# Pairs' value products and scores moved behind the second layer of their step, squares of h in PSUM in all steps, block sums amid the next step's gelu

## The chip, the cores and the metric

One core of one Trainium2 chip runs the whole program. The metric is the device time of one execution in microseconds; lower is better.

## The reference, cut to what matters

Attention over a window of 16 positions plus block summaries (block maxima of the keys, block means of the values), and on its output a two-layer network with a rational activation.

```python
# B=4, H=8, S=768, D=64, blocks of 32, window 16; 3072 tokens, d_model 512, d_ff 2048, fp32
k_sum = k.reshape(B, H, nb, block, D).max(axis=3)
v_sum = v.reshape(B, H, nb, block, D).mean(axis=3)
scores = concat(masked scale*q@k.T, scale*q@k_sum.T + log(block))
x = softmax(scores) @ concat(v, v_sum)            # then tokens x 512
h = x @ w_in
P = a0 + a1*h + a2*h*h + a3*h*h*h
Q = 1.0 + |b0|*|h| + |b1|*h*h
out = (P / (Q + 1e-6)) @ w_out
```

## The kernel before, in words

**Tiles.** The attention is cut into 48 halves of 64 queries; from half 16 on they come in pairs. The network runs over 6 groups of 512 tokens, and for each over 16 chunks of 128 hidden units. One chunk of one group is a *step*, number n = 16 g + fc, 0 to 95. Products in fp32 precision are made of three fp32r products of a high and a low part.

**One step n.** TensorE makes `h` (12 matmuls of 512 columns, `moe1`, L515), then the second layer `po` of an older step, n - 3 (12 matmuls, `moe2`, L596). Between the two lies the activation `gelu` (L531) in parts named by letters, which the text uses with the step's number behind them (c42):

- a, on ScalarE: `sq` (square of h) and `ta` (|h| scaled); b, on ScalarE: `tu` (linear in h). In steps where `sq` has no tile of its own it is written to `tq` in SBUF.
- c, on VectorE: `tq` from `sq` and `ta` (this is Q); d, on ScalarE: `ta` = ln, then exp.
- e, f, on VectorE: `tu` times h, twice; both read h in PSUM. i: `gh` = `tu` times `ta`. j and J: `tq` from `tq` and `gh`, then `tu` from `tu` and `tq`. k, on GpSimd (POOL): `gl` = `tu` times `ta`.

**PSUM.** Four banks hold `po`; two (`ps_h`) hold `h` and, in steps with a pair, the pair's value products `av`; two (`ps_a`) hold the pair's two score tiles `sc` and the tiles `sq`. `ta`, `tq`, `tu` have two buffers in SBUF each.

**Pairs.** Steps 14, 18, 22, ..., 74 (`halves`) each carry a pair: `both_scores` makes its `sc` tiles; `softmax` takes them off with 8 VectorE rows (`ss<-sc,mask`), 8 exponentials on ScalarE, reciprocals on VectorE and 8 scalings on GpSimd; one step later two VectorE transposes (`tb`) and a way through DRAM turn them; four steps later `both_values` makes `av`, ScalarE copies it (`x`, `xh`) and `xl` is formed. The output of a group is copied off by ScalarE (`o`) in steps 18, 34, 50, 66.

**Block sums.** For batches 2 and 3 `reduces` holds 8 VectorE reductions each (4 `ks`, 4 `vs`), one a step, in steps 20 to 29 and 37 to 53.

**Order.** Up to step 13 the order is a table of tokens. From step 14 on (`NSTRICT`, L734) the loop at the end issues step by step; TensorE keeps that order to the instruction, and the other engines' order comes from a list scheduler that goes by priority. All engines run their instructions in the order in which they then stand. All instructions of the loop bear line 113, that of the helper that records them, in the profile.

Of the kernel before, what the change touches and what calls it, by code (L numbers as in the profile page):

```python
# [12 lines left out]
AF = mybir.ActivationFunctionType  # L13
ALU = mybir.AluOpType
# [5 lines left out]
BLK, WIN = 32, 16  # L20
# [45 lines left out]
NSTRICT = NFC - 2  # L66
# [8 lines left out]
SQ_PS = "011001101001110"  # L75
# [5 lines left out]
NHALF = NT // HQ  # L81
# [3 lines left out]
def tile_kernel(ctx, tc, qw_in, kraw, kwin, vpad, vred, wio, a, b, cmask, cident, cavg, out):  # L85
# [37 lines left out]
    pe, dve, act, gps, syn = (Kept(e) for e in (nc.tensor, nc.vector, nc.scalar, nc.gpsimd, nc.sync))  # L123
# [65 lines left out]
    def value_sum(bi, c):  # L189
        vs, vr = vsum[bi], sums.pop(("v", bi, c))  # L190
        tc.keep_in_program_order(dve.tensor_reduce(vs[:, c, :], vr, axis=AX.X, op=ALU.add))
        if c == NVC - 1:
            dve.tensor_scalar_mul(vs, vs, 1.0 / BLK)

    def value_tiles(bi):
        vt = []
# [36 lines left out]
    def att_load(jj):  # L233
        bi, j = divmod(jj, NJ)
        assert jj < HPG + 2 or jj >= 2 * HPG + 2 or jj - 2 in scored
        syn.dma_start(out=qw[jj % 2], in_=qw_in[bi, j])
        syn.dma_start(out=kw[jj % 2][:, 0:NKC - 1], in_=kwin[bi, j])
# [277 lines left out]
    def moe1(g, fc, xh, xl):  # L515
        h = ps_h.tile([P, GT], F32, tag="h", name=f"h{g}_{fc}")
        k = 0
        wt = weights(fc)
        for i, x in ((0, xh), (0, xl), (1, xh)) if 0 < g * NFC + fc < NFC else ((0, xh), (1, xh), (0, xl)):
            if k:  # L520
                yield
            assert ("w" if i else "wh", fc) in order
            for cc in range(NCC):
                pe.matmul(h, wt[:, i, 0, cc * P:(cc + 1) * P], x[:, cc, :], start=(k == 0), stop=(k == 3 * NCC - 1))
                k += 1
        gh = gp.tile([P, GT], F32R, tag="gh", name=f"gh{g}_{fc}")
        gl = gp.tile([P, GT], F32R, tag="gl", name=f"gl{g}_{fc}")
        gelus[g * NFC + fc] = gelu(h, gh, gl, g, fc)
        queue.append((g, fc, (gh, gl)))

    def gelu(h, gh, gl, g, fc):  # L531
        ta = mp.tile([P, GT], F32, tag="ta", bufs=NTA, name=f"ta{g}_{fc}")
        tq = mp.tile([P, GT], F32, tag="tq", bufs=NTQ, name=f"tq{g}_{fc}")
        tu = mp.tile([P, GT], F32, tag="tu", bufs=NTU, name=f"tu{g}_{fc}")
        n = g * NFC + fc
        sq = tq

        product = n < NSTRICT and PRODUCT[n] == "1"

        def a():  # L540
            nonlocal sq
            if product:
                act.activation(ta, h, AF.Abs)
                act.activation(tq, ta, AF.Identity, scale=cs[:, 5:6], bias=cs[:, 4:5])
                return
            if n < start_of(NHALF - 1) + 4 and (n not in halves if n > NSTRICT else n < len(SQ_PS) and SQ_PS[n] == "1"):
                sq = ps_a.tile([P, GT], F32, tag="a", name=f"sq{g}_{fc}")
            act.activation(sq, h, AF.Square)
            act.activation(ta, h, AF.Abs, scale=cs[:, 4:5])

        def b():
            act.activation(tu, h, AF.Identity, scale=cs[:, 3:4], bias=cs[:, 2:3])

        def c():
            if product:
                gps.tensor_tensor(tq, tq, ta, op=ALU.mult)
                return
            dve.scalar_tensor_tensor(out=tq, in0=sq, scalar=cs[:, 5:6], in1=ta, op0=ALU.mult, op1=ALU.add)

        def d():  # L560
            act.activation(ta, tq, AF.Ln, bias=cs[:, 7:8])
            act.activation(ta, ta, AF.Exp, scale=-1.0)

        def e():
            dve.tensor_tensor(tu, tu, h, op=ALU.mult)

        def f():
            dve.scalar_tensor_tensor(out=tu, in0=tu, scalar=cs[:, 1:2], in1=h, op0=ALU.add, op1=ALU.mult)

        def i():  # L570
            dve.scalar_tensor_tensor(out=gh, in0=tu, scalar=cs[:, 0:1], in1=ta, op0=ALU.add, op1=ALU.mult)

        def j():
            dve.scalar_tensor_tensor(out=tq, in0=tq, scalar=C1 * SH, in1=gh, op0=ALU.add, op1=ALU.mult)
            dve.scalar_tensor_tensor(out=tu, in0=tu, scalar=cs[:, 0:1], in1=tq, op0=ALU.add, op1=ALU.subtract)

        def k():
            gps.tensor_tensor(gl, tu, ta, op=ALU.mult)

        return dict(a=a, b=b, c=c, d=d, e=e, f=f, i=i, j=j, k=k)  # L580
# [6 lines left out]
        if not parts:  # L587
            del gelus[step]

    def gelu_rest(step):  # L590
        for what in "abcdefijk":
            if what in gelus[step]:
                gelus[step].pop(what)()
        del gelus[step]

    def moe2(fc, po, gh, gl):  # L596
        wt = weights(fc)
        for t in range(TPG):
            ts_ = slice(t * P, (t + 1) * P)
            for i, (l, r) in enumerate(((gh, 0), (gh, 1), (gl, 0))):  # L600
                pe.matmul(po[t], l[:, ts_], wt[:, r, 1, :], start=(fc == 0 and i == 0),
                   stop=(fc == NFC - 1 and i == 2))
            yield

    def finish(g, po):
        for t in range(TPG):
            if g == NG - 1:
                o = gp.tile([P, DM], F32, tag="gl" if t % 2 else "gh", name=f"o{g}_{t}")
            else:
                o = (gp if t in OWN else pp).tile([P, DM], F32, tag="o" if t in OWN else "p", name=f"o{g}_{t}", bufs=2 if t in OWN else 4)  # L610
            if g == NG - 1 and t == TPG - 1:
                rows = out[g * GT + t * P:g * GT + (t + 1) * P, :]
                o2 = gp.tile([P, DM], F32, tag="gh", name=f"o{g}_{t + 1}")
                act.copy(o[:, 0:DM // 2], po[t][:, 0:DM // 2])
                dve.tensor_copy(o2[:, 0:DM // 2], po[t][:, DM // 2:])
                act.dma_start(out=rows[:, 0:DM // 2], in_=o[:, 0:DM // 2])
                syn.dma_start(out=rows[:, DM // 2:], in_=o2[:, 0:DM // 2])
                continue
            if g == NG - 1 and t % 2:
                dve.tensor_copy(o, po[t])  # L620
            else:
                act.copy(o, po[t])
            syn.dma_start(out=out[g * GT + t * P:g * GT + (t + 1) * P, :], in_=o)

    queue, out_tiles, gelus = [], [], {}

    def second_layer():
        g, fc, r = queue.pop(0)
        assert g * NFC + fc not in gelus
        if fc == 0:  # L630
            out_tiles[:] = [ps_o.tile([P, DM], F32, tag="o", name=f"po{g}_{t}") for t in range(TPG)]
        yield from moe2(fc, out_tiles, *r)
        if fc == NFC - 1:
            with tc.high_priority(offset=80):
                finish(g, out_tiles)
# [11 lines left out]
    def lead(chain, all_of=False):  # L647
        for _ in chain or ():
            if not all_of:
                return  # L650

    def start_of(jj):
        return EARLY_HALF[jj - HPG] if jj < 2 * HPG else NFC - 2 + 4 * ((jj - 2 * HPG) // 2)

    halves = {}
    for jj in range(HPG, NHALF):
        halves.setdefault(start_of(jj), []).append(jj)
    reduces, loads = {}, {}
# [68 lines left out]
    for s in sorted(gelus):  # L727
        gelu_rest(s)
# [5 lines left out]
    for step in range(NSTRICT, NG * NFC + LAG):  # L734
        g, fc = divmod(step, NFC)
        if g < NG:
            lead(moe1(g, fc, *x32[g]), True)
        if step in gelus:
            with tc.high_priority(offset=-15):
                gelu_rest(step)  # L740
        with tc.high_priority(offset=40):
            if step - 4 >= NFC - 2 and halves.get(step - 4):
                both_values(halves[step - 4][0])
            for jj in halves.get(step, ()):
                key_blocks(jj)
            if step in halves:
                chain = [softmax(jj, sc) for jj, sc in zip(halves[step], both_scores(halves[step][0]))]
            else:
                chain = ()
            for _ in range(5):  # L750
                for c in chain:
                    lead(c)
            for jj in halves.get(step - CROSS, ()):
                if jj >= 2 * HPG:
                    crossed(jj)
            for jj in halves.get(step - 1, ()):
                if jj >= 2 * HPG:
                    load_v(jj)
            for jj in halves.get(step, ()):
                if jj + 2 < NHALF:  # L760
                    att_load(jj + 2)
        lead(second_layer(), True)
        for f, *args in reduces.get(step, []) + loads.get(step, []):
            f(*args)


# [56 lines left out]
```

## Time and profile before

| what | value |
|---|---|
| runs before, median of 3 (lowest, highest) | 637.39 us (636.9, 637.84) |
| profiled execution: span | 636.9 us |
| TensorE busy | 620.4 us, 97% |
| VectorE busy | 568.5 us, 89% |
| ScalarE busy | 457.1 us, 72% |
| GpSimd busy | 256.9 us, 40% |
| granted TensorE clock | full in all slices |

The profiled execution's own time is the lowest of the three, 636.9 us, and its span is the same: nothing lies around the span that the sum has to add. A busy share is an average over the span; matmuls overlap, so TensorE's own pace is read from the starts of its matmuls.

### The profile page before, as it was taken

The numbers are of one execution on the slowest core, as the hardware profiler recorded it, in microseconds if no ns is written. First come the engines' busy times: TensorE is split into PE (matmuls) and PEld (weight loads), VectorE is DVE, ScalarE is ACT, GpSimd is POOL, SyncE is SP. The second block draws the span as 40 slices with busy tenths as digits, with TensorE's granted clock in tenths as the row PEclk, the third lists the DMA queues.
The fourth block names the chain that finished last, engine by engine and source line by source line (L and its number), as shares of the span: only waits on it lengthen the run. The fifth ranks groups of instructions, "written<-read, shape, count | busy, mean of one in ns | idle before, by whom it ended". The sixth has DMA issues, their size and how long they took to land.

```text
span 636.9 us, 11880 instructions
## 1 busy us (share of the span) xinstructions
PE 620.4 (97%) x4078; PEld 494.2 (78%) x4078; DVE 568.5 (89%) x1155; ACT 457.1 (72%) x1020; POOL 256.9 (40%) x344
## 2 busy tenths in 40 slices
PE   8899999999999999999999999999999999999997
PEld 4466777778788878888888777888888888888886
DVE  5799999999898999889988989988988989898885
ACT  3789999877867757767767768667777765656662
POOL 1366679654434336233143244243234242222221
PEclk9999999999999999999999999999999999999999
DMA  9977777413434434324423433323333120100001
GB/s 289 341 281 233 242 220 232 165 40 126 148 113 136 138 114 155 106 99 138 134 89 120 136 124 101 95 72 106 93 132 100 57 65 1 63 4 1 1 2 66
DMA packets 51752, 77.66 MB, mean 122 GB/s; under 512 B 6260, under 2 KB 33524, under 8 KB 49772
## 3 DMA queue, kind: packets, MB, share of 16 engines
q1 hardware_dynamic: 50412, 74.75, 36.2%
q0 software_dynamic: 560, 1.77, 1.4%
q8 instruction: 32, 0.52, 0.3%
q10 hardware_dynamic: 720, 0.38, 0.2%
q14 instruction: 28, 0.23, 0.1%
HBM read 60.33 MB, written 14.73 MB: 118 GB/s over the span
## 4 chain that ended last, share of the span: by engine, by line
PE 62%; DVE 21%; ACT 6%; DMA 5%; issue 3%; POOL 2%; DVEq 0%; POOLq 0%; ACTq 0%
PE po L113 29%; PE h L113 28%; DVE tu L113 6%; DVE tq L113 5%; PE av L113 3%; DVE gh L113 2%; PE sc L113 2%; DMA wr<-in_wio_dram 2%; DVE wr L113 2%; ACT ta L113 2%; DMA kres<-in_kraw_dram 1%; DVE ss L113 1%; POOL ss L113 1%; DMA w<-wr 1%; ACT ss L113 1%
## 5 line engine op out<-in xcount | busy, mean ns | idle before, releaser
L113 POOL TENSOR_TENSOR gl<-tu,ta 128x512 fp32r<-128x512 f32 x96 | 129.4, 1348 | 296.5 <-DVE tu L113 140.3
L113 ACT ACTIVATE ta<-tq,cs 128x512 f32<-128x512 f32 x96 | 69.8, 727 | 80.5 <-DVE tq L113 79.6
L113 PE MATMUL po<-wearly,gh 128*128 128x512 f32 x384 | 120.3, 394 | 0.7 <-ACT o L113 0.7
L113 PE MATMUL po<-w,gh 128*128 128x512 f32 x384 | 119.7, 393 | 0.0
L113 POOL TENSOR_SCALAR ss<-ss,sm 128x120 f32<-128x120 f32 x176 | 84.3, 497 | 41.6 <-DVE sm L113 40.7
L113 PE MATMUL h<-xh,wearly 128*128 128x512 f32 x384 | 97.8, 394 | 1.6 <-DVE tu L113 1.0
L113 PE MATMUL h<-xh,w 128*128 128x512 f32 x384 | 96.8, 391 | 1.4 <-DVE sm L113 0.9
L113 PEld LDWEIGHTS h<-xh,wearly 128*128 128x128 f32 x384 | 71.5, 188 | 18.2 <-ACT ta L113 1.0
L113 PEld LDWEIGHTS po<-wearly,gh 128*128 128x128 f32 x384 | 70.8, 188 | 18.0 <-ACT o L113 2.4
L113 PEld LDWEIGHTS h<-xh,w 128*128 128x128 f32 x384 | 71.5, 188 | 17.0 <-ACT ta L113 1.3
L113 DVE SCALAR_TENSOR_TENSOR gh<-tu,cs,ta 128x512 fp32r<-128x512 f32 x96 | 73.8, 768 | 10.9 <-ACT ta L113 1.4
L113 PEld LDWEIGHTS po<-w,gh 128*128 128x128 f32 x384 | 71.2, 188 | 15.7 <-issue 1.1
L113 ACT ACTIVATE ss<-ss,sm 128x120 f32<-128x120 f32 x188 | 71.7, 385 | 12.2 <-DVE sm L113 12.2
L113 ACT ACTIVATE tu<-h,cs 128x512 f32<-128x512 f32 x96 | 74.7, 778 | 0.5 <-PE h L113 0.5
L113 PE MATMUL po<-w,gl 128*128 128x512 f32 x192 | 74.9, 390 | 0.0
L113 PE MATMUL po<-wearly,gl 128*128 128x512 f32 x192 | 74.8, 390 | 0.0
L113 DVE SCALAR_TENSOR_TENSOR tu<-tu,cs,tq 128x512 f32<-128x512 f32 x96 | 72.2, 753 | 2.6
L113 DVE SCALAR_TENSOR_TENSOR tu<-tu,cs,h 128x512 f32<-128x512 f32 x96 | 71.1, 741 | 2.2
L113 DVE SCALAR_TENSOR_TENSOR tq<-tq,gh 128x512 f32<-128x512 f32 x96 | 66.6, 694 | 2.7
L113 ACT ACTIVATE ta<-h,cs 128x512 f32<-128x512 f32 x95 | 64.6, 680 | 4.8 <-POOL gl L113 4.8
L113 DVE TENSOR_TENSOR tu<-tu,h 128x512 f32<-128x512 f32 x96 | 64.9, 676 | 0.1
L113 ACT ACTIVATE ta<-ta 128x512 f32<-128x512 f32 x96 | 60.8, 633 | 2.7
(92 smaller groups left out, 917.3 us busy)
## 6 DMA issues: line engine op xcount, KB each, us to landing
wr<-in_wio_dram SPq DMA_DIRECT2D x15, 1024.0 KB
cross<-tb SPq DMA_DIRECT2D x32, 256.0 KB
vw<-in_vpad_dram SPq DMA_DIRECT2D x42, 192.0 KB
kw<-in_kwin_dram SPq DMA_DIRECT2D x40, 192.0 KB
pts<-cross SPq DMA_DIRECT2D x96, 64.0 KB
out_dram<-o SPq DMA_DIRECT2D x23, 256.0 KB
qw<-in_qw_dram SPq DMA_DIRECT2D x40, 128.0 KB
kr<-in_kraw_dram SPq DMA_DIRECT2D x12, 384.0 KB
```

The source lines that it names most:

```text
L113: out = getattr(self.engine, name)(*args, **kw)
```

## The change

In the loop from step 14 on, the second layer now comes ahead of the pair's `both_values` and `both_scores`. `sq` gets a PSUM tile in every step after 14 (up to 77); in the step behind a pair, b comes first, then `ta`, and `sq` last. The block sums of step t are issued in step t + 1, between f and i. The scaling of the block means goes from VectorE to GpSimd.

```diff
         if c == NVC - 1:
-            dve.tensor_scalar_mul(vs, vs, 1.0 / BLK)
+            gps.tensor_scalar(vs, vs, 1.0 / BLK, 1.0, op0=ALU.mult, op1=ALU.mult)
...
-            if n < start_of(NHALF - 1) + 4 and (n not in halves if n > NSTRICT else n < len(SQ_PS) and SQ_PS[n] == "1"):
+            if n < start_of(NHALF - 1) + 4 and (n > NSTRICT or n < len(SQ_PS) and SQ_PS[n] == "1"):
                 sq = ps_a.tile([P, GT], F32, tag="a", name=f"sq{g}_{fc}")
-            act.activation(sq, h, AF.Square)
+            late = n > NSTRICT and n - 1 in halves
+            if not late:
+                act.activation(sq, h, AF.Square)
             act.activation(ta, h, AF.Abs, scale=cs[:, 4:5])
+            if late:
+                act.activation(sq, h, AF.Square)
...
-    def gelu_rest(step):
-        for what in "abcdefijk":
+    def gelu_rest(step, parts="abcdefijk"):
+        for what in parts:
             if what in gelus[step]:
                 gelus[step].pop(what)()
-        del gelus[step]
+        if not gelus[step]:
+            del gelus[step]
...
-        if step in gelus:
-            with tc.high_priority(offset=-15):
-                gelu_rest(step)
+        with tc.high_priority(offset=-15):
+            if step in gelus:
+                gelu_rest(step, "bacdef" if step - 1 in halves else "abcdef")
+            for f, *args in reduces.get(step - 1, []):
+                f(*args)
+            if step in gelus:
+                gelu_rest(step, "ijk")
+        lead(second_layer(), True)
         with tc.high_priority(offset=40):
...
-        lead(second_layer(), True)
-        for f, *args in reduces.get(step, []) + loads.get(step, []):
+        for f, *args in loads.get(step, []):
             f(*args)
```

Where instructions stand, at two places. In the names, `h2_10` is h of group 2, chunk 10, which is step 42; `sc30`, `ss30`, `sm30` belong to half 30; ISA rows that read `sc` are the softmax's first rows.

VectorE at pair step 42, before, from c42 to c43:

```order
L113 SCALAR_TENSOR_TENSOR tq2_10_3613<-tq2_10_3613,cs_98,ta2_10_3612 128x512
L113 TENSOR_TENSOR tu2_10_3614<-tu2_10_3614,h2_10_3597 128x512
L113 TENSOR_TENSOR xl3_3063<-x28_3644,xh3_3062 128x4x128
L113 ISA ss30_3666,sm30_3667<-sc30_3648,mask_96 128x120
...
L113 SCALAR_TENSOR_TENSOR tu2_10_3614<-tu2_10_3614,cs_98,h2_10_3597 128x512
L113 SCALAR_TENSOR_TENSOR gh2_10_3610<-tu2_10_3614,cs_98,ta2_10_3612 128x512
L113 SCALAR_TENSOR_TENSOR tq2_10_3613<-tq2_10_3613,gh2_10_3610 128x512
...
L113 SCALAR_TENSOR_TENSOR tu2_10_3614<-tu2_10_3614,cs_98,tq2_10_3613 128x512
L113 STREAM_TRANSPOSE tb30_3747<-ss30_3666 128x4x4x32
L113 SCALAR_TENSOR_TENSOR tq2_11_3732<-sq2_11_3734,cs_98,ta2_11_3731 128x512
```

The same place in the changed program:

```order
L113 SCALAR_TENSOR_TENSOR tu2_9_3572<-tu2_9_3572,cs_98,tq2_9_3571 128x512
L113 TENSOR_TENSOR tu2_10_3619<-tu2_10_3619,h2_10_3602 128x512
L113 SCALAR_TENSOR_TENSOR tu2_10_3619<-tu2_10_3619,cs_98,h2_10_3602 128x512
L113 TENSOR_REDUCE ks3_3170<-kr3_2_3326 128x24
L113 SCALAR_TENSOR_TENSOR gh2_10_3615<-tu2_10_3619,cs_98,ta2_10_3617 128x512
L113 TENSOR_TENSOR xl3_3092<-x28_3663,xh3_3091 128x4x128
L113 ISA ss30_3685,sm30_3686<-sc30_3667,mask_96 128x120
...
L113 SCALAR_TENSOR_TENSOR tq2_10_3618<-tq2_10_3618,gh2_10_3615 128x512
...
L113 SCALAR_TENSOR_TENSOR tu2_10_3619<-tu2_10_3619,cs_98,tq2_10_3618 128x512
L113 RECIPROCAL sm30_3686<-sm30_3686 128x4
L113 SCALAR_TENSOR_TENSOR tq2_11_3739<-sq2_11_3742,cs_98,ta2_11_3738 128x512
L113 TENSOR_TENSOR tu2_11_3740<-tu2_11_3740,h2_11_3723 128x512
```

c42 itself stands just ahead of the first of these rows, which is J41. The softmax's first rows have moved from between e42 and f42 to behind f42, a block sum and i42.

ScalarE at the same place, before, from the ln of step 42 on:

```order
L113 ACTIVATE ta2_10_3612<-tq2_10_3613,cs_98 128x512
L113 ACTIVATE ta2_10_3612<-ta2_10_3612 128x512
L113 ACTIVATE ss30_3666,sm30_3667<-ss30_3666,sm30_3667 128x120 x4
L113 ACTIVATE ss31_3672,sm31_3673<-ss31_3672,sm31_3673 128x120 x4
L113 ACTIVATE sm30_3667<-sm30_3667 128x4
L113 ACTIVATE sm31_3673<-sm31_3673 128x4
L113 ACTIVATE sq2_11_3734<-h2_11_3716 128x512
L113 ACTIVATE ta2_11_3731<-h2_11_3716,cs_98 128x512
L113 ACTIVATE tu2_11_3733<-h2_11_3716,cs_98 128x512
```

In the changed program:

```order
L113 ACTIVATE ta2_10_3617<-tq2_10_3618,cs_98 128x512
L113 ACTIVATE ta2_10_3617<-ta2_10_3617 128x512
L113 COPY x28_3663<-av28_3646 128x512
L113 CAST xh3_3091<-x28_3663 128x4x128
L113 ACTIVATE ss30_3685,sm30_3686<-ss30_3685,sm30_3686 128x120 x4
L113 ACTIVATE ss31_3691,sm31_3692<-ss31_3691,sm31_3692 128x120 x2
L113 ACTIVATE sm30_3686<-sm30_3686 128x4
L113 ACTIVATE ss31_3691,sm31_3692<-ss31_3691,sm31_3692 128x120 x2
L113 ACTIVATE tu2_11_3740<-h2_11_3723,cs_98 128x512
L113 ACTIVATE ta2_11_3738<-h2_11_3723,cs_98 128x512
L113 ACTIVATE sq2_11_3742<-h2_11_3723 128x512
```

The copies of `av` have moved behind the exponential of step 42, and the square of step 43 stands last of three instead of first, behind the same 8 exponentials.

The second place is steps 16 to 18 (`h1_0`, `h1_1`, `h1_2`). ScalarE in the changed program:

```order
L113 ACTIVATE sq1_0_1851<-h1_0_1833 128x512
L113 ACTIVATE ta1_0_1848<-h1_0_1833,cs_98 128x512
L113 ACTIVATE tu1_0_1850<-h1_0_1833,cs_98 128x512
L113 ACTIVATE sq1_1_1894<-h1_1_1876 128x512
L113 ACTIVATE ta1_1_1891<-h1_1_1876,cs_98 128x512
L113 ACTIVATE tu1_1_1893<-h1_1_1876,cs_98 128x512
L113 ACTIVATE ta1_0_1848<-tq1_0_1849,cs_98 128x512
...
L113 ACTIVATE sq1_2_1940<-h1_2_1922 128x512
L113 COPY o0_0_1965<-po0_0_788 128x512
...
L113 COPY o0_3_1974<-po0_3_791 128x512
L113 ACTIVATE ta1_2_1937<-h1_2_1922,cs_98 128x512
L113 ACTIVATE tu1_2_1939<-h1_2_1922,cs_98 128x512
```

Before, the ln and the exp of step 16 stood ahead of `sq1_1`, and the four output copies stood amid the exponentials behind step 18's own part d. VectorE there, in the changed program:

```order
L113 SCALAR_TENSOR_TENSOR gh1_0_1846<-tu1_0_1850,cs_98,ta1_0_1848 128x512
L113 SCALAR_TENSOR_TENSOR gh1_1_1889<-tu1_1_1893,cs_98,ta1_1_1891 128x512
L113 SCALAR_TENSOR_TENSOR tq1_0_1849<-tq1_0_1849,gh1_0_1846 128x512
L113 SCALAR_TENSOR_TENSOR tq1_1_1892<-tq1_1_1892,gh1_1_1889 128x512
L113 SCALAR_TENSOR_TENSOR tu1_0_1850<-tu1_0_1850,cs_98,tq1_0_1849 128x512
L113 SCALAR_TENSOR_TENSOR tu1_1_1893<-tu1_1_1893,cs_98,tq1_1_1892 128x512
L113 SCALAR_TENSOR_TENSOR tq1_2_1938<-sq1_2_1940,cs_98,ta1_2_1937 128x512
```

Steps 16 and 17 now go through i, j and J in turns, behind c, e, f of both; before, J16 came ahead of e17.

What the changed program's instructions wait for: in each pair step from 18 on the second `sc` tile takes the buffer of that step's own `sq`, and so waits for its c. The `h` behind a pair waits for f of the pair's step (steps 23, 35, 39 and each later one up to 75) or for the copy `x` of `av` (steps 19, 27, 31); before, it waited for `x` in all of them. `av` waits for f of the step before, now as before.

## Rows read from the trace of the kernel before

**Rows 1.** The page's head and its part 1: busy us, share of the span and instructions of each engine.

```profile
span 636.9 us, 11880 instructions
PE 620.4 (97%) x4078; PEld 494.2 (78%) x4078; DVE 568.5 (89%) x1155; ACT 457.1 (72%) x1020; POOL 256.9 (40%) x344
```

**Rows 2.** Busy time by stretch: the stretch and its length in us, then the busy time of each engine with its instructions, the granted clock, the DMA share and GB/s.

```profile
169.00:365.00 196.00, 194.79 (x1292) 160.08 (x1291) 179.16 (x382) 140.43 (x328) 73.29 (x119) 1.00 0.40 125
...
390.00:525.00 135.00, 134.98 (x865) 110.74 (x864) 120.99 (x252) 96.28 (x229) 50.64 (x82) 1.00 0.28 89
525.00:600.00 75.00, 75.00 (x358) 61.95 (x358) 65.86 (x85) 45.61 (x73) 19.33 (x14) 1.00 0.04 15
```

**Rows 3.** Waits of TensorE's matmuls from 136 to 640 us: who waited for whom, us in total, times, longest.

```profile
PE av L113 <- DVE tu L113: 2.1, 3, 1.2
PE po L113 <- ACT o L113: 0.7, 1, 0.7
```

**Rows 4.** Timeline of TensorE (start, length, instruction): the first matmul of h in steps 19, 58, 62 and 75.

```profile
168.91 0.39 PE L113 MATMUL h<-xh,wearly 128*128 128x512 f32 x1
404.88 0.39 PE L113 MATMUL h<-xh,w 128*128 128x512 f32 x1
428.94 0.39 PE L113 MATMUL h<-xh,w 128*128 128x512 f32 x1
509.18 1.98 PE L113 MATMUL h<-xh,w 128*128 128x512 f32 x8
```

**Rows 5.** Timeline of TensorE at pair step 42, whose h ends where the first row begins.

```profile
309.58 1.15 PE L113 MATMUL av<-pts,vw 120*64 120x64 f32 x32
...
311.64 0.73 PE L113 MATMUL po<-wearly,gh 128*128 128x512 f32 x2
...
314.50 1.29 PE L113 MATMUL h<-xh,w 128*128 128x512 f32 x5
...
317.23 0.61 PE L113 MATMUL po<-w,gh 128*128 128x512 f32 x2
```

**Rows 6.** Timeline of VectorE at the same step (c42, xl, first of 8 softmax rows, f42, i42, J42, first transpose), and c58; in brackets the idle time ahead and what ended it.

```profile
312.04 1.24 DVE L113 SCALAR_TENSOR_TENSOR tq<-tq,cs,ta 128x512 f32<-128x512 f32 x1
...
313.80 0.68 DVE L113 TENSOR_TENSOR xl<-x,xh 128x512 fp32r<-128x512 f32 x1
314.40 0.27 DVE L113 CUSTOM_DVE_ANT_0 ss<-sc,mask 128x120 f32<-128x120 f32 x1
...
316.02 0.74 DVE L113 SCALAR_TENSOR_TENSOR tu<-tu,cs,h 128x512 f32<-128x512 f32 x1
316.89 0.75 DVE L113 SCALAR_TENSOR_TENSOR gh<-tu,cs,ta 128x512 fp32r<-128x512 f32 x1
...
318.44 0.72 DVE L113 SCALAR_TENSOR_TENSOR tu<-tu,cs,tq 128x512 f32<-128x512 f32 x1
320.46 0.71 DVE L113 STREAM_TRANSPOSE tb<-ss 128x512 f32<-128x512 f32 x1 [1.30 <-POOL ss L113]
...
409.01 1.60 DVE L113 SCALAR_TENSOR_TENSOR tq<-tq,cs,ta 128x512 f32<-128x512 f32 x1 [0.39 <-ACT ta L113]
```

**Rows 7.** Timeline of ScalarE there: ln of step 42, the first of 8 exponentials, the two small rows behind them, and the three reads of h43.

```profile
313.31 0.72 ACT L113 ACTIVATE ta<-tq,cs 128x512 f32<-128x512 f32 x1 [0.65 <-DVE tq L113]
...
314.71 0.40 ACT L113 ACTIVATE ss<-ss,sm 128x120 f32<-128x120 f32 x1
...
317.76 0.33 ACT L113 ACTIVATE sm<-sm 128x4 f32<-128x4 f32 x2
318.00 0.58 ACT L113 ACTIVATE sq<-h 128x512 f32<-128x512 f32 x1
318.51 0.67 ACT L113 ACTIVATE ta<-h,cs 128x512 f32<-128x512 f32 x1
319.08 0.77 ACT L113 ACTIVATE tu<-h,cs 128x512 f32<-128x512 f32 x1
```

**Rows 8.** Groups of VectorE instructions from 136 to 540 us, shapes kept apart: count, busy us, mean ns of one, idle time ahead.

```profile
L113 DVE SCALAR_TENSOR_TENSOR tq<-sq,cs,ta 128x512 f32<-128x512 f32 x49 | 36.3, 741 | 5.3 <-ACT ta L113 5.2
L113 DVE SCALAR_TENSOR_TENSOR tq<-tq,cs,ta 128x512 f32<-128x512 f32 x18 | 23.4, 1301 | 3.2 <-ACT ta L113 3.2
...
L113 DVE TENSOR_REDUCE vs<-vr 96x32 f32<-96x1024 f32 x8 | 9.6, 1203 | 0.0
...
L113 DVE TENSOR_REDUCE ks<-kr 128x24 f32<-128x768 f32 x8 | 7.5, 941 | 0.0
```

**Rows 9.** Timeline: k41 on GpSimd as c42 starts, and k15 on GpSimd with i16 on VectorE.

```profile
311.43 1.30 POOL L113 TENSOR_TENSOR gl<-tu,ta 128x512 fp32r<-128x512 f32 x1 [4.00 <-DVE tu L113]
158.65 1.29 POOL L113 TENSOR_TENSOR gl<-tu,ta 128x512 fp32r<-128x512 f32 x1 [3.54 <-ACT sq L113]
159.27 1.22 DVE L113 SCALAR_TENSOR_TENSOR gh<-tu,cs,ta 128x512 fp32r<-128x512 f32 x1
```

**Rows 10.** Timeline of steps 14 to 18: last 28 of the 32 matmuls of sc in step 14, then J14, ta16, c18.

```profile
139.95 1.04 PE L113 MATMUL sc<-kw,qw 64*64 64x120 f32 x28 [0.42 <-DVE tq L113]
152.90 0.74 DVE L113 SCALAR_TENSOR_TENSOR tu<-tu,cs,tq 128x512 f32<-128x512 f32 x1
155.14 0.69 ACT L113 ACTIVATE ta<-h,cs 128x512 f32<-128x512 f32 x1 [2.40 <-POOL gl L113]
165.44 0.74 DVE L113 SCALAR_TENSOR_TENSOR tq<-tq,cs,ta 128x512 f32<-128x512 f32 x1
```

## The prediction

> **What bounds the kernel now.** I read busy shares first, then the stretches, the waits and two timelines. TensorE is busy for 97% of the span, VectorE for 89% [rows 1]. By stretch, TensorE hardly stops from 169 us on, at the full granted clock throughout [rows 2]; VectorE is busy for 91% of the first of these stretches and 90% of the second, so two engines are near their limit. Without a hole, four steps with one pair take 428.94 - 404.88 = 24.06 us from h58 to h62 [rows 4]. From h19 to h75 lie 14 such periods, 336.84 us; they took 509.18 - 168.91 = 340.27, so the holes there are 3.4 us. Of these the waits name 2.1 us of `av` for f (VectorE's `tu`) and 0.7 of `po` for the output copies [rows 3]. A better order of TensorE's work cannot give more than this 3.4 and the 0.4 of `sc` ahead of step 19 [rows 10]; for a loss there is no such bound.
>
> The next question is how late VectorE may be. I measure its lateness s as the start of c behind the end of its h. At step 42, h ends at 309.58 [rows 5] and c starts at 312.04 [rows 6], so s = 2.46; at step 58, h starts at 404.88 [rows 4], takes 2.8 (the 2.72 of h43, 314.50 to 317.23 [rows 5], and somewhat under 0.1 at a pair) and c starts at 409.01 [rows 6], so s = 1.3. Lateness thus rises and falls with VectorE's load, and TensorE goes on as long as nothing that it needs is behind it.
>
> **What the change does with holes.** Now `po`, which needs only an older step, stands behind h, and `av`, `sc` come 2.7 us later (2.72 for 12 matmuls, 317.23 - 314.50 [rows 5]). `av`'s wait for f of the step before, and `po`'s for the copies, then have that time as cover. I book the whole 3.4 as gained, with bounds 2.8 (what the waits name) and 3.4.
>
> **What it does with VectorE's work.** With `sq` in PSUM, c took 741 ns (49 cases), with `sq` in SBUF 1301 ns (18) [rows 8]. The cause is in the rows: c42, both of whose inputs lie in SBUF, starts amid k41 on GpSimd (311.43 + 1.30 = 312.73) and ends at 313.28 [rows 6, 9], 0.55 behind it. By the means, 15 pair steps save 15 x 0.56 = 8.4 us of VectorE's time. But i too has two SBUF inputs: i16 took 1.22 while k15 ran [rows 9]. In the new order i of the step behind next stands behind J of a pair's neighbour, inside k, once in nearly every period: I add back 0.55 a period, and so the saving is nearly gone. It costs nothing only if k is past by then.
>
> The Trainium skill ("SBUF — State Buffer", section "SBUF: two separate sides") calls the port pair shared by VectorE and GpSimd an exclusive lock, held for a whole instruction, also against a VectorE operation with two SBUF inputs; the trace agrees (1.22 instead of 0.75). Against the change, "Perfetto Trace Analysis" of the Trainium skill, section "Optimizing Scalar/DVE Operations", gives VectorE about 65 ns more per instruction on PSUM than on SBUF; by it the 15 moved c's would cost 1.0 us more as an estimate. The trace does not bear it out: c18 from SBUF with the port free took 0.74 [rows 10], as from PSUM.
>
> The scaling of the block means, two small instructions, goes to GpSimd, busy 40% [rows 1]: nothing, while GpSimd's idle time covers it; else a few tenths. The DMA way of the transposed weights starts some 2 us later in its step, against four steps (24.06) until `av` reads: nothing.
>
> **What it does with waits.** Two are new. The second `sc` tile waits for c of its own step: `sc` can begin 2.72 + 1.1 behind the end of h (`av` takes 1.15, a little of it overlapped [rows 5]), and its wait comes behind 4 of 32 matmuls [rows 10], so at about 3.95; c needs 0.74, so s may be 3.1 at most. And h of the next step waits for f; a pair adds 24.06 - 8 x 2.72 = 2.3 to a period, so h could begin at 5.0, and with c, e, f (three rows of some 0.7, 2.15) s may be 2.85, or 2.2 where J of the step before stands between c and e, as in the order at step 42. Before, h waited for the copy of `av` only, and at step 42 s was already 2.46.
>
> And VectorE gets later. In the new order the first softmax row stands behind f, a block sum and i. The eight exponentials are ahead of all three reads of the next h on ScalarE, `sq` last. By the rows, the exponentials take 317.76 - 314.71 = 3.05, the small rows 0.24, then `sq`, `ta`, `tu` 0.5, 0.6 and 0.77 [rows 7]: c43 can start 0.3 + 3.05 + 0.24 + 1.85 = 5.4 behind the first softmax row. In this time VectorE has 8 rows (316.02 - 314.40 = 1.6 [rows 6]), j and J (1.5) and a reciprocal: 3.2 to 3.3. So it idles 2.2 us a period; before, f and i (1.55) lay there too and the idle was 1.30, behind GpSimd, ahead of the transpose [rows 6].
>
> From 390 to 525 us, with no block sum, VectorE was busy 120.99 / 135 x 24.06 = 21.6 us a period, from 169 to 365 us 22.0 [rows 2] with about 12 block sums of 0.94 and 1.20 [rows 8], so 20.5 without. After the saving of 0.56 and the 0.55 added, 20.5 to 21.6 remain; I take 21.2. With the idle 2.2 this is 23.4, and each block sum adds 1.0 (they overlap their neighbours a little). Against 24.06, a period with two block sums makes VectorE 1.3 us later, one with three 2.3, one with none 0.7 earlier.
>
> **The sum.**
> - Ahead of step 19: `sc` of step 14 loses its wait (0.4 [rows 10]), but steps 16 and 17 now run through i, j, J in turns and four output copies (2.3 us) stand ahead of `ta18`. `ta16` waited for a `gl` already [rows 10], and does again, later. c18 came at 165.44, 12.5 behind J14 [rows 10]; by the rows that now stand ahead it comes up to 3.6 later. h18 and its `po` hide a part: +2.1 at h19 with the 0.4 taken off (bounds -0.4 and 3.6).
> - Holes: -3.4.
> - New stalls, step by step from s = 2 at step 22, each stall being what s exceeds its limit by (a stall holds all back, so s falls by it): with the eight block sums of steps 20 to 29, steps 26, 30, 34: 1.3 + 1.5 + 1.2 = 4.0; with the eight of 37 to 53, steps 42, 46, 50, 54: 1.3 + 1.3 + 0.7 + 0.9 = 4.2; without any, steps 58, 62, 74: 0.9 + 0.7 + 0.5 = 2.1. Together +10.3 (bounds 0, if s never reaches a limit, and 15, if each of the 15 pair steps 18 to 74 loses 1.0).
> - Head and tail have the same order in both: 0; they cover nothing new.
>
> Sum: +2.1 - 3.4 + 10.3 = +9.0 on 636.9, 645.9. The median stands 0.5 above the profiled execution: 646.4.
>
> **Rivals.**
> (1) *VectorE's relief wins.* The 8.4 us come free as booked and i meets no k. VectorE's 21.6 lose 0.56 net, and if its idle stays at before's 1.3, a period with two block sums is 21.0 + 1.3 + 2.0 = 24.3 and others less; s stays under 2.2. Then there are no new stalls, and step 16 costs nothing: 637.4 - 3.4 - 0.4 = 633.6. It decides if s at pair steps stays at or below 2.2. For it: s was 1.3 at step 58. Against: 2.46 at 42, and the exponentials.
> (2) *Nothing to be seen.* Stalls of some 1.5 and 2 at the start eat the 3.4: 637.4.
> (3) *Half.* The idle is 1.7 instead of 2.2, as GpSimd's scalings or transposes fill it: growth 0.8, stalls 5, sum +3.7: 641.
> (4) *More.* Port waits at j too, or f late in every pair: 15 of stalls and 3.6 at the start, less 3.4: 652.6.
>
> **How the numbers follow.** Stalls as worked out, give or take a third: 0.47. Rival (3): 0.25; (4): 0.06; (2): 0.08; (1): 0.14, as my walk goes by starts of single rows and a shift of 0.5 in s at each pair would undo most of it. About 0.2% is what a measurement of this kernel can tell from no change, that is 636.1 to 638.7. Faster 0.14, same 0.08, slower 0.78. The likeliest case alone spans 643 to 650. The range leaves out rival (1) and half of (4), and holds 637 to 652.
>
> **What would show it.** In the changed kernel's trace: no `av` waits for f (holes, right); waits of the second `sc` for `tq` and of h for `tu` behind pairs, about 10 us together (stalls, right); VectorE idle some 2 us ahead of the c behind a pair, ended by ScalarE (idle, right; under 1.5, rival (1) or (3)); c at 0.74 in all pair steps but i at 1.2 in a dozen; h19 at about 171. I am wrong if c at pair steps starts within 2.2 us of the end of h with block sums about, since then neither new wait is ever reached.

## The result, and the profile after

The changed kernel takes 641.69 us (median of 5 runs, 641.27 to 642.43), the kernel before 637.63 beside it: 1.0064 times as long, with an interval of 1.0052 to 1.0077. It is slower, as forecast, but by 4.1 us where 9.0 were forecast (646.4). The page and the waits of TensorE from 136 to 640 us, of the changed kernel:

```profile
span 640.0 us, 11923 instructions
PE 619.5 (97%) x4078; PEld 494.7 (77%) x4078; DVE 561.0 (88%) x1153; ACT 457.8 (72%) x1020; POOL 257.4 (40%) x346
```

```profile
PE h L113 <- DVE tu L113: 4.3, 8, 1.2
PE sc L113 <- issue: 1.7, 1, 1.7
PE h L113 <- ACT x L113: 1.1, 2, 0.7
```

The waits of [rows 3], `av` for f and `po` for the output copies, are gone. In their place h waits for f (`tu`) eight times, for the copy of `av` twice, and `sc` once, for a c (below). VectorE is busy 7.5 us less than in [rows 1], in a longer span: work has gone from it, and time has not.

One statement ahead of the prediction does not hold, that nothing lies around the span. Every execution of which both numbers are known takes 1.8 us more than its span (the profiled one of the changed kernel: span 640.0, time 641.83). The profiled execution of before, span 636.9, was therefore not the run of 636.9 us but a slower one, near 638.7. Where it lost that shows at h14, up to which all programs here have the same order: it starts at 136.29 before and at 135.23 after, and in two executions of one and the same kernel (e8 below) at 136.38 and 134.60. So a difference of some 1 us ahead of h14 belongs to the execution. Behind h14 the traces differ by 3.1 + 1.06, some 4.2 us, which is about the 4.1 of the medians.

By stretch, from the starts of h in the timeline of TensorE; the last column is what the steps h22 to h74 with a pair take above the 7.6 us that one takes without a stall:

```
kernel               median  ratio [interval]          h14-h19  h19-h75  h75-h79  pair stalls
before               637.6   1                          32.61   340.28    23.07   -
changed              641.69  1.0064 [1.0052, 1.0077]    34.33   341.34    24.37    4.4
e1_order             643.79  1.0101 [1.0086, 1.0116]    33.47   343.84    24.66    7.0
e2_sums_end          643.25  1.0095 [1.0078, 1.0112]    34.32   342.33    24.01    5.5
e3_sq_sbuf           641.34  1.0066 [1.0051, 1.0081]    33.50   341.52    24.65    4.6
e5_vs_on_dve         642.41  1.0067 [1.0053, 1.0080]    34.34   342.35    24.03    3.7
e6_rows_first        637.09  0.9999 [0.9989, 1.0008]    34.29   336.73    23.78    0
e7_start             640.88  1.0041 [1.0027, 1.0055]    32.97   341.27    24.04    4.4
e8_both              636.06  0.9968 [0.9955, 0.9980]    32.93   336.74    23.78    0
e8_again             635.40  0.9967 [0.9956, 0.9978]    32.97   336.74    23.78    0
e9_small_sums        643.18  1.0074 [1.0057, 1.0091]    34.31   343.28    24.38    3.5
e10_both_sq_sbuf     635.44  0.9967 [0.9955, 0.9979]    33.05   336.97    23.65    0.1
e11_both_sums_end    635.90  0.9971 [0.9961, 0.9982]    32.92   336.92    23.78    0.1
```

The ratios are to the kernel before run beside each (medians 637.4 to 638.0). In the traces of e5 and e9, h19 to h75 holds 1.6 us of a slower clock (last section).

So these 4.2 us are: +1.72 in steps 14 to 19; +1.06 from h19 to h75, made of the 3.43 of holes that went and of 4.5 that came; +1.30 from h75 to h79; +0.1 behind.

**Pair step 42 after.** Timeline of VectorE: i40, c42, f42, the block sum, i42, xl, the first softmax row, J42, a reciprocal, c43.

```profile
306.30 1.22 DVE L113 SCALAR_TENSOR_TENSOR gh<-tu,cs,ta 128x512 fp32r<-128x512 f32 x1
...
313.24 0.74 DVE L113 SCALAR_TENSOR_TENSOR tq<-sq,cs,ta 128x512 f32<-128x512 f32 x1
...
315.27 0.75 DVE L113 SCALAR_TENSOR_TENSOR tu<-tu,cs,h 128x512 f32<-128x512 f32 x1
315.93 0.94 DVE L113 TENSOR_REDUCE ks<-kr 128x24 f32<-128x768 f32 x1
316.80 0.74 DVE L113 SCALAR_TENSOR_TENSOR gh<-tu,cs,ta 128x512 fp32r<-128x512 f32 x1
317.46 0.68 DVE L113 TENSOR_TENSOR xl<-x,xh 128x512 fp32r<-128x512 f32 x1
318.06 0.27 DVE L113 CUSTOM_DVE_ANT_0 ss<-sc,mask 128x120 f32<-128x120 f32 x1
...
320.28 0.74 DVE L113 SCALAR_TENSOR_TENSOR tu<-tu,cs,tq 128x512 f32<-128x512 f32 x1
320.95 0.17 DVE L113 RECIPROCAL sm<-sm 128x4 f32<-128x4 f32 x1
323.37 0.75 DVE L113 SCALAR_TENSOR_TENSOR tq<-sq,cs,ta 128x512 f32<-128x512 f32 x1 [2.26 <-ACT sq L113]
```

TensorE and ScalarE at the same place (`sc`, the next h; first exponential, then the square of step 43):

```profile
314.32 1.05 PE L113 MATMUL sc<-kw,qw 64*64 64x120 f32 x32
316.07 1.21 PE L113 MATMUL h<-xh,w 128*128 128x512 f32 x4 [0.70 <-DVE tu L113]
```

```profile
318.38 0.40 ACT L113 ACTIVATE ss<-ss,sm 128x120 f32<-128x120 f32 x1 [1.85 <-DVE sm L113]
...
322.76 0.58 ACT L113 ACTIVATE sq<-h 128x512 f32<-128x512 f32 x1
```

The scores are there at 315.37, but the first row comes at 318.06, behind f, the sum, i and xl. ScalarE waits 1.85 us for it; its square of step 43 then ends at 323.34, 5.3 behind the first row (5.4 forecast), and VectorE idles 2.26 (2.2 forecast). h43 waits for f42, which ends at 316.02: s was 2.82 (313.24 less the end of h42 at 310.42), 0.6 above the limit of 2.2, and the wait is 0.70. i40 takes 1.22 beside k39, which runs on GpSimd from 305.68 to 306.97. All of it was forecast; what was not is how little it adds up to.

### The profile page after: what moved, and what is told of

Same layout as the page of the kernel before. It is cut to its first block, busy times and chain, and to the rows that moved or that the text cites. A ratio compares the mean times of both kernels' runs of the same rounds, so it can differ in the third digit from the quotient of the medians.

```text
span 640.0 us, 11923 instructions
## 1 busy us (share of the span) xinstructions
PE 619.5 (97%) x4078; PEld 494.7 (77%) x4078; DVE 561.0 (88%) x1153; ACT 457.8 (72%) x1020; POOL 257.4 (40%) x346
## 4 chain that ended last, share of the span: by engine, by line
PE 38%; DVE 36%; issue 9%; ACT 8%; DMA 4%; POOL 4%; DVEq 0%; SPq 0%; POOLq 0%; ACTq 0%
PE h L113 18%; PE po L113 17%; DVE tu L113 14%; DVE tq L113 9%; DVE gh L113 5%; ACT ss L113 4%; POOL ss L113 2%; DVE tb L113 2%; DMA wr<-in_wio_dram 2%; DMA kres<-in_kraw_dram 1%; DVE wr L113 1%; DVE ss L113 1%; ACT ta L113 1%; DVE w L113 1%; PE vf L113 1%
## 5 line engine op out<-in xcount | busy, mean ns | idle before, releaser
L113 PE MATMUL po<-wearly,gh 128*128 128x512 f32 x384 | 118.7, 390 | 0.0
L113 PE MATMUL h<-xh,w 128*128 128x512 f32 x384 | 98.1, 394 | 5.1 <-DVE tu L113 2.8
L113 PE MATMUL h<-xh,wearly 128*128 128x512 f32 x384 | 99.1, 397 | 3.1 <-DVE tu L113 2.5
L113 ACT ACTIVATE ss<-ss,sm 128x120 f32<-128x120 f32 x188 | 71.7, 385 | 33.6 <-DVE sm L113 33.5
L113 DVE SCALAR_TENSOR_TENSOR gh<-tu,cs,ta 128x512 fp32r<-128x512 f32 x96 | 80.1, 835 | 11.0 <-ACT ta L113 3.2
L113 PEld LDWEIGHTS h<-xh,w 128*128 128x128 f32 x384 | 70.9, 188 | 21.9 <-DVE tu L113 4.2
L113 DVE SCALAR_TENSOR_TENSOR tq<-sq,cs,ta 128x512 f32<-128x512 f32 x71 | 52.4, 739 | 15.8 <-ACT sq L113 13.6
```

The costliest lines, as they stand in the source:

```text
L113: out = getattr(self.engine, name)(*args, **kw)
```

## The experiments

Two theories at first. **A**: the loss comes with the new order, through late softmax rows, late exponentials and an idle VectorE. **The rivals**: it comes from the squares or the sums, or from i's port waits.

**e1_order.** The kernel before with the order alone:

```diff
                 gelu_rest(step)
+        lead(second_layer(), True)
         with tc.high_priority(offset=40):
...
-        lead(second_layer(), True)
         for f, *args in reduces.get(step, []) + loads.get(step, []):
```

> The kernel before with one part of the change: the second layer ahead of the pair's products; squares, block sums and the scaling of the means as before. Theory A (the loss comes with the order: softmax rows come late, so the exponentials stand ahead of the next h's reads and VectorE idles 2 us or more a period, and h waits for f behind pairs): the 3.4 us of holes go, steps 14 to 19 cost about 1.7, stalls behind pairs some 4 to 5 and 1.2 at step 78: about 641 to 642. Rival B (the order is the useful part, the loss comes from squares in PSUM and the moved block sums): holes gone and little else, about 635 to 636.

643.79: the order alone is worse than the whole change, and worse than the 641 to 642 of theory A. Rival B falls. The stalls are 7.0 us, above A's 4 to 5, and with the 336.84 of 14 periods without a hole they make the 343.84 from h19 to h75. Steps 14 to 19 took 0.9 more than before, where A had 1.7. The rest of the change therefore earns some 2 us back.

**e2_sums_end.** The changed kernel, sums back at the end of their step:

```diff
-            for f, *args in reduces.get(step - 1, []):
-                f(*args)
...
-        for f, *args in loads.get(step, []):
+        for f, *args in reduces.get(step, []) + loads.get(step, []):
```

> The changed kernel with the block sums back at the end of their own step. Theory A1 (a block sum between f and i lies where i would wait for its exponential or for the port that GpSimd's k holds, and so costs less than its length): i at 1.2 us in more steps, later by up to 0.5 us for each of some 10 sums, about 643. Rival A2 (the sum between f and i holds the softmax rows up by 0.9 in the six pair steps that have one, and so the exponentials and the next c): without it 640 to 641.

643.25, as A1 has it (the interval's low end, 1.0078, lies just above the changed kernel's high end of 1.0077), with 5.5 us of stalls. But A1's reason does not hold: i took more than 1 us in 14 of 56 rows, against 13 in the changed kernel. Moving the sums is worth 1.6 us by the medians (the trace of e2, its fastest execution, shows 1.0 of it from h19 to h75); by which way is open. The rows allow that a sum ahead of e and f, as here, makes f late for h, and one behind f does not.

**e3_sq_sbuf.** The changed kernel with the squares of pair steps in SBUF:

```diff
-            if n < start_of(NHALF - 1) + 4 and (n > NSTRICT or n < len(SQ_PS) and SQ_PS[n] == "1"):
+            if n < start_of(NHALF - 1) + 4 and (n not in halves if n > NSTRICT else n < len(SQ_PS) and SQ_PS[n] == "1"):
...
-            late = n > NSTRICT and n - 1 in halves
+            late = False
...
-                gelu_rest(step, "bacdef" if step - 1 in halves else "abcdef")
+                gelu_rest(step, "abcdef")
```

> The changed kernel with the squares of pair steps in SBUF as before, and the plain order of a, b behind a pair. Theory C (what c gains at a pair step, 0.56 us, i loses one step on, so squares in PSUM are worth nothing): within 0.5 us of the changed kernel, 641.2 to 642.2, with c at 1.2 and more in pair steps and i at 1.2 in few steps. Rival D (the gain of c is real and the stalls come from a near miss): VectorE 0.5 us later a period, 12 of 15 pair steps lose 0.4 more, about 646.

641.34: theory C by the time, and wrong in its mechanism. VectorE's groups from 186 to 527 us (count, busy us, mean ns), of e3, then c of pair steps in the kernel before:

```profile
L113 DVE SCALAR_TENSOR_TENSOR gh<-tu,cs,ta 128x512 fp32r<-128x512 f32 x56 | 48.9, 873 | 7.8 <-ACT ta L113 2.7
...
L113 DVE SCALAR_TENSOR_TENSOR tq<-tq,cs,ta 128x512 f32<-128x512 f32 x14 | 10.4, 745 | 0.0
```

```profile
L113 DVE SCALAR_TENSOR_TENSOR tq<-tq,cs,ta 128x512 f32<-128x512 f32 x14 | 18.9, 1349 | 2.2 <-ACT ta L113 2.2
```

Before, c of a pair step started inside k of the step before in 12 of 14 cases. In e3 it reads the square from SBUF too, and takes 745 ns, as it starts ahead of that k in all 14. In 10 of them k starts 0.25 us behind c, and now it is k that takes longer, 1.63 to 1.65 us instead of 1.3. Step 42 of e3, k41 and c42:

```profile
314.17 1.63 POOL L113 TENSOR_TENSOR gl<-tu,ta 128x512 fp32r<-128x512 f32 x1 [3.77 <-DVE tu L113]
```

```profile
313.92 0.74 DVE L113 SCALAR_TENSOR_TENSOR tq<-tq,cs,ta 128x512 f32<-128x512 f32 x1
```

So most of the 8.4 us of relief that were booked for PSUM come with the order itself: in e1, the order alone, c of pair steps took 886 ns in the mean, and four of the 14 still 1.21 to 1.31 us. The squares' new place gives nothing on top that the times show, and at one place it costs: in e1 and e3 the second `sc` of step 18 does not wait for c18, and h14 to h19 takes 33.5 us, 0.8 less than in the changed kernel. i waits for the port in e3 as in the changed kernel (873 ns and 875, 762 before). The rule of the Trainium skill ("SBUF — State Buffer", section "SBUF: two separate sides"), a lock that whichever starts first holds for the length of one instruction, fits: c ahead of k takes 0.74, and a k that starts during it waits; c inside k takes 1.2 and more.

**e6_rows_first.** The changed kernel, in pair steps from 22 on with the 8 rows directly behind f; `xl` (`low`), the sum, i, j, J follow:

```diff
...
+        rows_first = step in halves and step > NSTRICT + 4
...
+            if rows_first:
+                strict.add(dve)
+                for c in chain:
+                    lead(c)
+                strict.discard(dve)
+                if low:
+                    low()
+                with tc.high_priority(offset=-15):
+                    for f, *args in reduces.get(step - 1, []):
+                        f(*args)
+                    gelu_rest(step, "ijk")
```

> The changed kernel with the 8 softmax rows of a pair (from step 22 on) put right behind f of their step, ahead of xl, the block sum and i. Theory A (the exponentials, late because the rows are late, keep VectorE idle for 2 us a period, and this is what makes c late): c behind a pair about 2 us earlier, VectorE's wait for ScalarE's square under 0.7 a period, stalls of h behind pairs (4.3 us in the changed kernel) under 1: 636 to 637.5. Rival E (the port waits of i, 14 rows at 1.2 us in the changed kernel, make it late; the idle time is slack): the stalls stay, 641 to 642.

637.09, a gain of 4.6 us (4.1 by the ratios), and every stall behind a pair from step 22 on is gone. Step 42 there, first row and c43:

```profile
314.27 0.28 DVE L113 CUSTOM_DVE_ANT_0 ss<-sc,mask 128x120 f32<-128x120 f32 x1 [0.78 <-PE sc L113]
...
319.58 0.75 DVE L113 SCALAR_TENSOR_TENSOR tq<-sq,cs,ta 128x512 f32<-128x512 f32 x1
```

c43 starts 5.42 behind h43's start (314.16) instead of 7.30 (316.07 to 323.37). Rival E falls: i still waits for the port (842 ns in the mean, 10 rows above 1 us). VectorE's waits from 186 to 527 us, of the changed kernel and of e6:

```profile
DVE tq L113 <- ACT sq L113: 13.6, 11, 2.3
DVE tb L113 <- POOL ss L113: 10.8, 12, 1.8
DVE sm L113 <- ACT sm L113: 6.9, 6, 2.5
```

```profile
DVE ss L113 <- PE sc L113: 15.0, 14, 1.4
DVE tq L113 <- ACT sq L113: 6.4, 10, 0.9
```

VectorE now waits 15.0 us for TensorE's scores, which is harmless: TensorE is what it waits for, and has no hole.

**e7_start.** The changed kernel with ScalarE's gelu kept in the text's order in steps 15 to 21:

```diff
+        kept = (act,) if NSTRICT < step < NSTRICT + 8 else ()
...
+            strict.update(kept)
             if step in gelus:
                 gelu_rest(step, "bacdef" if step - 1 in halves else "abcdef")
...
+            strict.difference_update(kept)
```

> The changed kernel with one thing kept in the text's order: ScalarE's gelu in steps 15 to 21, so that ln and exp of step 16 stand ahead of the square of step 17 again, and the four output copies of step 18 behind its exp. Theory F (the chain k16, ta18, c18, second sc tile costs steps 14 to 19 the 1.7 us that they take longer than before): h19 comes 1 to 1.7 us earlier behind h14, all else the same, about 640 to 640.7. Rival G (the delay sits earlier, in the two transposes of step 15 that wait for GpSimd): steps 14 to 19 stay at 34.3 us, 641.7.

640.88, with h14 to h19 in 32.97 instead of 34.33: theory F, its gain of 1.36 inside the 1 to 1.7, the time a little above the 640 to 640.7. The edit moves the ln of step 16 and the output copies together, so it does not tell their shares. The chain in the changed kernel, on ScalarE, VectorE and TensorE (output copies, ta18, c18, second `sc` tile):

```profile
163.50 2.62 ACT L113 COPY o<-po 128x512 f32<-128x512 f32 x4
167.02 0.69 ACT L113 ACTIVATE ta<-h,cs 128x512 f32<-128x512 f32 x1 [0.90 <-POOL gl L113]
```

```profile
167.74 0.75 DVE L113 SCALAR_TENSOR_TENSOR tq<-sq,cs,ta 128x512 f32<-128x512 f32 x1 [1.89 <-ACT ta L113]
```

```profile
168.59 1.04 PE L113 MATMUL sc<-kw,qw 64*64 64x120 f32 x28 [1.66 <-issue]
```

The last one's releaser is not named; it starts 0.10 behind the end of c18. The `gl` is k16, late because J16 stood behind step 17's c, e, f, i and j.

**e8_both, e8_again.** e6 (from step 18 on) and e7 together.

> The changed kernel with both: softmax rows right behind f in pair steps, and ScalarE's order kept in steps 15 to 21. If the two losses are separate, their gains add: 637.1 less 1 to 1.7, about 635.5 to 636, 0.2 to 0.3% below the kernel before. If rows ahead in step 18 already cure the start, or the kept order costs later steps, it stays at 637.

> The kernel with softmax rows behind f and ScalarE's order kept in steps 15 to 21 once more, beside the next two on one chip: 0.9968 of the kernel before again, about 635.5 to 636.5.

636.06 and 635.40, 0.9968 and 0.9967 of the kernel before: the two gains add, and this version is faster than both kernels. From h19 to h75 it takes 336.74, the 14 unhindered periods of the prediction.

**e9_small_sums.** The changed kernel with sums over 2 elements of each block:

```diff
+        few = 2 if bi > 1 else BLK
-        ins = dve.tensor_reduce(ksum[bi][:, pr, :], kr.rearrange("p (n k) -> p n k", k=BLK), axis=AX.X, op=ALU.max)
+        ins = dve.tensor_reduce(ksum[bi][:, pr, :], kr.rearrange("p (n k) -> p n k", k=BLK)[:, :, 0:few], axis=AX.X, op=ALU.max)
...
-        tc.keep_in_program_order(dve.tensor_reduce(vs[:, c, :], vr, axis=AX.X, op=ALU.add))
+        tc.keep_in_program_order(dve.tensor_reduce(vs[:, c, :], vr[:, :, 0:2], axis=AX.X, op=ALU.add))
```

> The changed kernel with the 16 block sums of batches 2 and 3 taken over 2 elements of each block instead of 32: part of the sums is left out, all else is computed. Theory H (each block sum adds its 1.0 us to VectorE's need, as in the prediction's sum): steps 22 to 54 need 2.0 us less a period, their stalls (3.3 us) go, about 638. Rival I (between f and i a sum lies where VectorE would wait anyway for the exponential or the port, so it costs much less than its length; what the prediction had too large is this term): stalls stay at the level of the steps without sums, 0.25 us a pair step, and the time at 640 to 641.

643.18: H falls, and I is not right either, since nothing at all was gained. Busy time from c22 to c54, columns as in [rows 2], of the changed kernel and of e9:

```profile
190.72:386.60 195.88, 193.73 (x1284) 158.63 (x1283) 175.04 (x375) 140.29 (x329) 73.07 (x118) 1.00 0.40 124
```

```profile
192.46:389.16 196.70, 194.94 (x1286) 159.40 (x1285) 168.67 (x375) 140.96 (x329) 72.52 (x118) 1.00 0.39 122
```

VectorE is busy for 6.4 us less, in 0.8 us more. But the run does not test less work alone. With the sums short, the scheduler put j, and at some pair steps J, ahead of the softmax rows as well: at pair steps 22 to 50 the first row comes 2.54 us behind the end of f in the mean, later than the 2.22 of the changed kernel. What the sums gave up was taken by other rows ahead of the softmax, and VectorE idled for the rest. A further stall of 1.0 us at step 32 is of this kind: h33 starts at 256.28, 0.05 behind the end of f31, whose square came late behind the exponentials of step 30. The trace also holds the 1.6 us of a slower clock, ahead of this stretch.

**e5_vs_on_dve.** The changed kernel, `dve.tensor_scalar_mul` for the scaling of the means:

> The changed kernel with the scaling of the block means on VectorE as before: two rows of 0.2 us more there. As costed at nothing, 641.5 to 642; if the move matters, above 642.2.

642.41 is above the line of 642.2, but the kernel before beside it was slower too (637.99, against 637.63): by the ratios, 1.0067 and 1.0064 with intervals that overlap almost whole, there is no difference that this measurement can tell, as costed.

**e10, e11.** e8_both with the squares of pair steps in SBUF, and with the sums at the end of their step (the edits of e3 and e2).

> The kernel of e8_both with the squares of pair steps in SBUF. With the rows ahead, c at pair steps already stands at its earliest (1.4 us behind the end of h, limit 2.2 to 2.85). Theory J (a chain through VectorE and ScalarE sets the pace, and VectorE's work counts for little): c of 1.2 us at some pair steps costs nothing, within 0.5 us of e8_both. Rival K (VectorE's total work counts): 7 to 8 us more of it bring stalls back, 638 or more.

> The kernel of e8_both with the block sums at the end of their own step. Theory J: nothing is near a limit, within 0.5 us of e8_both. Rival K: sums ahead of the next e and f bring f past its limit at some of six pair steps, 637 to 638.

635.44 and 635.90 beside 635.40: no difference, as theory J has it. c at pair steps starts at 1.4 to 2.4 us behind h, inside the limits that the prediction gave, and then neither the squares' place nor that of the sums counts. Rival K is hardly tested by it: VectorE's busy time rose by 2.5 us in e10 (564.1 against 561.6) and by 0.5 in e11, not by 7 to 8, since c took longer at 5 of 14 pair steps only.

## Why the prediction was wrong in size

**Right.** The sign; the holes (3.43 gone, 3.4 booked); steps 14 to 19 (+1.72; +2.1 forecast, by the chain that e7 undid); the new wait of h and where it strikes (the new wait of the second `sc` struck in step 18 alone): stalls of 0.3 to 0.8 at steps 26, 30, 42, 46, 54, 62 and 74, none at 38, 66 and 70 (34, 50 and 58, forecast with 0.7 to 1.2, have 0.2 and less); the idle time from the first softmax row to the next c (2.15 us in the mean of 14 pair steps, 2.2 forecast) and its cause, which e6 took away with all stalls (0.57 there); the scaling at nothing.

**Wrong: the term of the new stalls.** +10.3 was forecast for the pair steps to 74, 4.4 came (3.2 in steps 26 to 54, where 8.2 were forecast, and 1.2 in steps 58 to 74, where 2.1 were). The step that failed is VectorE's need per period: "I take 21.2. With the idle 2.2 this is 23.4, and each block sum adds 1.0", so 25.15 us with the 14 sums that lie in the 8 periods from c22 to c54, and 23.6 with the one that lies in the 5 periods from c54 to c74. In the changed kernel c22 starts at 190.72, c54 at 386.60 and c74 at 508.71: 24.48 us a period in the first stretch and 24.42 in the second. The first stretch's busy time is shown under e9; the second's is

```profile
386.60:508.71 122.11, 120.92 (x815) 99.32 (x816) 104.70 (x228) 86.97 (x204) 43.88 (x73) 1.00 0.31 95
```

So VectorE was busy for 21.9 us a period and idle for 2.6 in the first, and for 20.9 and 3.5 in the second. Booked were 22.95 and 2.2, and 21.4 and 2.2. In the first the busy time was put 1.1 too high: the 21.2 stood as one value for two stretches that had 20.5 and 21.6 [rows 2], and the first of these has less still, 20.3, as 14 sums and not about 12 lie in its window. In the second the idle time was put 1.3 too low: 2.5 of it lies between the first softmax row and the next c, and 1.0 elsewhere, mostly ahead of i, which the sum put at nothing. A period that is 0.67 too long makes 5.4 us in 8 periods, about what the stalls of steps 26 to 54 fell short by; as slack refunds nothing, the second error, which lies the other way, does not take it back.

The period hardly follows the work, nor does it in e2 (24.48, 24.41) and e3 (24.48, 24.43), and e9, busy for 0.8 us less a period, keeps 24.59. What sets the 24.4 is rather a chain of waits: c, exponential, i, rows, eight exponentials, three reads, next c (5.3 to 5.8 us from the first row on, in all 14 pair steps), and then three steps in which c catches up some 2 us in all (s from 4.41 at step 43 to 2.35 at step 46). That the rows are a link of it, e6 shows. That it is the same with and without sums goes with where the first row stands: 2.24 us behind the end of f in the mean of pair steps 22 to 54, and 2.32 in steps 58 to 74, where j at four of five, and J at two, stands in a sum's place. The catching up is argued from the timeline only.

**Wrong: the cause of one gain.** That PSUM would make c quicker at pair steps: e3 has the same 0.74 from SBUF, by starting ahead of k. The sum was not hurt, since i's waits (+6.3 us over 56 rows, 49.0 against 42.7) were rightly set against it.

**Missed: step 78.** The tail from step 75 on was costed at nothing. But the pair of step 74 has its `av` in step 78, and h79 waits for f78 as the others do, on TensorE and, ahead of it, f78 on VectorE:

```profile
535.27 2.12 PE L113 MATMUL h<-xh,w 128*128 128x512 f32 x8 [1.22 <-DVE tu L113]
```

```profile
534.47 0.75 DVE L113 SCALAR_TENSOR_TENSOR tu<-tu,cs,h 128x512 f32<-128x512 f32 x1
```

In trace terms: +1.7 - 3.4 + 4.5 + 1.3 = +4.1, where +2.1 - 3.4 + 10.3 + 0 was written. Rival (3) has the right time, 641, but not the reason: the idle did not shrink.

**The change as a whole.** Its order costs 6.3 us alone (e1), its sums give about 2 of that back in that order (e2), its squares and the scaling nothing that could be measured. With rows and ScalarE's order repaired, the whole gains some 2 us (0.9967), and neither the squares nor the sums have a part in it that could be measured (e10, e11); the order without both was not run so.

## What to carry to other kernels

When a transfer between engines is moved behind other work on one queue, look at the other end of its chain: here the scores came 2.7 us later, and the consumer's queue then had three more instructions ahead of them, which cost more than the holes that the move closed. Price a new wait by the chain through all engines, from one c to the next, not by the sum of one engine's busy time; where the sum is used, use it for each stretch with that stretch's own numbers, and with all of the engine's idle time. And a resource conflict that the trace of before shows (c inside k) may change sides by the shift alone: here c came to start ahead of k, and k waited.

## What was not expected of the hardware

In the profiled executions of e5 and e9 TensorE's granted clock fell behind the hole of 1.7 us in `sc` of step 18. In e5, by stretch (length, TensorE's busy time with its matmuls, granted clock, DMA share, GB/s):

```profile
167.00:169.00 2.00, 0.35 (x13) 1.00 0.47 135
169.00:171.00 2.00, 2.00 (x29) 0.81 0.74 236
171.00:173.00 2.00, 2.00 (x6) 0.50 0.89 260
173.00:175.00 2.00, 2.00 (x8) 0.84 0.13 47
175.00:177.00 2.00, 2.00 (x10) 1.00 0.00 1
```

The clock is at the lower of its two levels (0.50, 1.2 GHz) for over 2 us, and step 19 takes 7.19 us instead of 5.59: the hole is paid for almost twice. In the profiled executions of the changed kernel, e2 and e6 the same hole is there and the clock stays at 1.00. Of the executions whose mean granted clock is on record it is 0.997 or less in 7 of the 27 of the five kernels that have this hole (the changed kernel, e2, e5, e6, e9), and in none of the 37 of the other variants or the 37 of the kernel before; so the fall goes with the hole. Why it comes in one execution and not in another stays open. e8, which has no such hole (0.60 at most), is free of it.
